# A float64-weight repair moved from VectorE to ScalarE, and a tile of their own for the first two chunks' results

## The chip, the cores and the metric

The kernel runs on one core of one Trainium2 chip. The metric is device time in microseconds (us) of one execution. Three executions of the kernel before took 899.41, 894.22 and 908.81 us, so the median is 899.41 us. The engines are TensorE (PE, with its weight loads as PEld), VectorE (DVE), ScalarE (ACT), GpSimd (POOL) and SyncE (SP), which issues most DMAs. Each runs its own instructions strictly in the order in which the program holds them.

## The reference

Three stages are chained. `S` is 576, the head dimension 64, with 4 batches of 8 heads; the 2304 tokens have 512 columns.

```python
# 1. attention: a pooled one (mean over 4 positions) and a local one (|i - j| < 4), added
out_d = sm_attn(q_d, k_d, v_d); out_up = np.repeat(out_d, 4, axis=2)
scores = np.where(mask, scale * q @ k.T, -1e9); out_local = softmax(scores) @ v
x = (out_up + out_local) as rows of (2304, 512)
# 2. a dense layer with a gate, w_in (512, 2048), w_out (2048, 512)
h = x @ w_in
g = np.where(h >= 1, h, np.where(h <= -1, 0.0, (h + 1) ** 2 / 4))
x = g @ w_out
# 3. eight experts: tokens are given out greedily by logits = x @ w_gate, 288 to each
for e in range(8):
    out[mask_e] = np.maximum(x[mask_e] @ w1[e], 0) @ w2[e]
```

`w_in` and `w_out` arrive as float64. Each is turned into float32 on the chip, by integer work on its two 32-bit words.

## The kernel before

**Tiling.** Attention runs per pair of heads: 16 pairs, each with a pooled part (`pooled`) and two local parts (`local`, g = 0 and 1). Results go to a buffer in device memory, `x_cols`. The dense layer takes the tokens in chunks of 256: seven chunks (c = 0 to 6) and a last piece of 512. For each chunk `x_cols` is loaded into the tile `xio`, split into a rounded high part and a low part (tiles `xts0` and `xts1`, even and odd chunks), and multiplied by 16 tiles of `w_in`; gated; and multiplied by 16 tiles of `w_out`. Each product takes three matmuls, high by high, high by low, low by high. In the trace the first product reads `bk<-xts,wi` and the second `bk<-wo,ghi` and `bk<-wo,glo`. Then come the routing and the experts.

**Weights.** There are 32 weight tiles, 16 of each matrix. `prep(w, f)` makes one of them ready. `scale64` lets ACT read the high words as floats times 2^-111 into a temporary `t` (or `gar`), and lets POOL reduce the high words, in place, to their sign. DVE then takes the top three bits of the low words, ors them onto the sign, shifts `t` left by three and ors again: two integer instructions, the second and third lines of

```python
        lw, hw = words(w, f)
        V.scalar_tensor_tensor(hw, lw, 29, hw, op0=OP.logical_shift_right, op1=OP.bitwise_or)
        V.scalar_tensor_tensor(ti, ti, 3, hw, op0=OP.logical_shift_left, op1=OP.bitwise_or)
```

`parts` then lets ACT copy `t` to the rounded high part, and DVE or POOL subtract to get the low part. For `w_out`, `gate_rows` also turns the tile on PE and multiplies it by the gate's weights (`bk<-wgk,rows`).

**Chunks 0 and 1** are special: `up` and `down` run them f by f while attention and weights are still being made, with the results in four PSUM banks (second products 512 wide). `flush_first` copies a chunk's results to `xio`, sends them to `x_rows`, and multiplies them by the gate's weights. From chunk 2 on, second products are 256 and 264 wide, and the first one waits until both flushes have emptied their banks.

**What sets the order.** The program is written by a planner: the functions above are generators, and `run` picks the next step by estimated engine times and by priorities (`PRIO`). What a step waits for (a tile's slot, a bank, a mark of another step) is its `need(...)`. A step given as a dictionary of engines and costs goes to the engine that the planner takes to be cheapest. Where the planner expects PE to be idle ahead of the first chunk, it puts matmuls on a bank of no use, `bk<-cst`, to keep PE busy. The tile `xio` has one slot, and the chunks' loads and all flushes share it; ahead of chunk 0 the attention uses it as scratch space.

Lines in the trace: 120 and 124 are PE's matmuls and transposes, 128 is ACT, 141 is DVE and POOL, 106 is SP's DMA. These are helpers, so instructions are told apart by their tiles.

## Time and profile before

| | |
|---|---|
| median of three runs | 899.41 us |
| the profiled execution | 900.66 us |
| its span in the trace, first to last instruction | 898.5 us |
| PE busy | 858.7 us (96%) |
| DVE busy | 514.9 us (57%) |
| ACT busy | 463.1 us (52%) |
| POOL busy | 439.2 us (49%) |

The span is 2.2 us shorter than the time of that execution, which is 1.25 us above the median of the runs. Busy PE time includes the matmuls on the useless bank, and a matmul that runs at half clock counts as busy for twice as long. The shares are means over stages with different limits, so they are read by stretch.

### The profile page before, as it was taken

The page shows a single profiled execution, that of the slowest core. Times are in us where ns is not written, and L with a number is a line of the kernel's source. Part 1 is how long each engine was busy: PE and PEld are TensorE (multiplying, and loading weights), DVE is VectorE, ACT ScalarE, POOL GpSimd, SP SyncE. Part 2 cuts the span into 40 slices and gives each one's busy share as a digit, 9 for nine tenths or more (in the row PEclk, how much of TensorE's full clock was granted, in tenths as well). Part 3 has the DMA queues.
Part 4 walks back from the last instruction along what each step waited for, and adds up shares of the span by engine and source line. Part 5 has one row for each costly group of instructions (what it writes and reads, how often), then busy time and mean ns, then how long its engine had stood idle before and what let it go on. Part 6 is the DMA issues. An engine that isn't in the chain of part 4 may idle for free.

```text
span 898.5 us, 20588 instructions
## 1 busy us (share of the span) xinstructions
PE 858.7 (96%) x7891; PEld 777.8 (87%) x7891; DVE 514.9 (57%) x1469; ACT 463.1 (52%) x1295; POOL 439.2 (49%) x498
## 2 busy tenths in 40 slices
PE   7879999989899999999999999998999999999995
PEld 6768888878899999999999877777988998989995
DVE  6788989876454543423221564475576766767520
ACT  5877786776466666544444551032343443544641
POOL 3765477654244544444444210033855756657741
PEclk9999999999899999999999999997999999999998
DMA  9755455223222310301000000053433544436620
GB/s 308 232 176 185 139 179 194 88 61 111 89 64 70 103 42 15 95 1 49 1 25 1 30 1 6 1 207 126 145 122 128 183 140 152 150 101 209 208 84 27
DMA packets 39010, 95.41 MB, mean 106 GB/s; under 512 B 4992, under 2 KB 17152, under 8 KB 38912
## 3 DMA queue, kind: packets, MB, share of 16 engines
q1 hardware_dynamic: 35840, 84.66, 28.8%
q0 software_dynamic: 3072, 9.44, 3.4%
q8 instruction: 62, 1.02, 0.5%
q14 instruction: 36, 0.29, 0.1%
HBM read 79.92 MB, written 14.16 MB: 105 GB/s over the span
## 4 chain that ended last, share of the span: by engine, by line
PE 72%; DVE 8%; DMA 7%; issue 5%; ACT 4%; POOL 2%; SPq 1%; POOLq 0%; DVEq 0%; ACTq 0%
PE bk L120 70%; PE bk L124 3%; DMA stg<-in_w_dram 2%; DVE gar L141 1%; DMA vw<-in_vw_dram 1%; ACT gar L128 1%; DVE raw L141 1%; DMA v<-in_v_dram 1%; DMA x_rows<-xio 1%; POOL wo L141 1%; DMA x_cols<-x 1%; POOL out_dram L1116 1%; SPq L106 1%; DVE t L141 1%; DMA xg<-x_rows,idx 1%
## 5 line engine op out<-in xcount | busy, mean ns | idle before, releaser
L120 PE MATMUL bk<-xts,wi 128*128 128x256 f32 x1344 | 184.8, 288 | 5.3 <-ACT gar L128 3.7
L120 PEld LDWEIGHTS bk<-xts,wi 128*128 128x128 f32 x1344 | 170.6, 192 | 9.4 <-ACT gar L128 5.1
L120 PE MATMUL bk<-wo,ghi 128*128 128x256 f32 (+2 forms) x768 | 161.8, 309 | 0.0
L128 ACT ACTIVATE gar<-bk,halves 128x256 f32<-128x256 f32 x224 | 93.8, 471 | 91.0 <-PE bk L120 85.4
L141 DVE SCALAR_TENSOR_TENSOR gar<-gar 128x256 f32<-128x256 f32 x112 | 57.4, 513 | 115.7 <-ACT gar L128 115.4
L120 PEld LDWEIGHTS bk<-wo,ghi 128*128 128x128 f32 x768 | 115.9, 190 | 4.6 <-issue 0.4
L141 POOL TENSOR_TENSOR glo<-gar,ghi 128x256 fp32r<-128x256 f32 x86 | 65.8, 771 | 86.4 <-ACT ghi L128 71.5
L141 POOL TENSOR_TENSOR wi<-stg,wi 128x512 fp32r<-128x512 f32 x51 | 64.7, 1297 | 69.4 <-DMA stg<-in_w_dram 43.0
L120 PE MATMUL bk<-wo,glo 128*128 128x256 f32 (+2 forms) x384 | 90.3, 303 | 0.2 <-DVE glo L141 0.2
L141 POOL TENSOR_TENSOR gar<-gar 128x256 f32<-128x256 f32 x64 | 49.6, 775 | 72.4 <-DVE gar L141 47.0
L141 POOL TENSOR_TENSOR wo<-stg,wo 128x512 fp32r<-128x512 f32 x50 | 65.6, 1335 | 37.6 <-ACT wo L128 37.3
L120 PEld LDWEIGHTS bk<-wo,glo 128*128 128x128 f32 x384 | 62.1, 189 | 3.6 <-DVE glo L141 0.9
L128 ACT ACTIVATE ghi<-gar 128x256 fp32r<-128x256 f32 x112 | 46.7, 417 | 34.9 <-POOL gar L141 19.5
L120 PE MATMUL bk<-xT,wi 128*128 128x288 f32 x384 | 60.8, 311 | 0.1
L120 PE MATMUL bk<-hT,wi 128*128 128x288 f32 x384 | 60.5, 304 | 0.0
L128 ACT ACTIVATE wi<-stg 128x1024 fp32r<-128x1024 f32 x32 | 33.6, 1056 | 51.4 <-DMA stg<-in_w_dram 51.4
L120 PE MATMUL bk<-hT,wo 128*128 128x288 f32 x384 | 58.8, 302 | 0.0
L120 PE MATMUL bk<-xT,wo 128*128 128x288 f32 x384 | 58.4, 302 | 0.1
L128 ACT ACTIVATE lt<-lt,lmx 128x64 f32<-128x64 f32 x160 | 53.8, 342 | 8.9 <-DVE lmx L141 8.7
L120 PEld LDWEIGHTS bk<-xT,wi 128*128 128x128 f32 x384 | 54.4, 197 | 0.8 <-DVE xT L141 0.3
L120 PEld LDWEIGHTS bk<-xT,wo 128*128 128x128 f32 x384 | 52.0, 188 | 1.0 <-DVE xT L141 0.6
L120 PEld LDWEIGHTS bk<-hT,wi 128*128 128x128 f32 x384 | 52.1, 188 | 0.7
(189 smaller groups left out, 1669.2 us busy)
## 6 DMA issues: line engine op xcount, KB each, us to landing
stg<-in_w_dram SPq DMA_DIRECT2D x64, 512.0 KB
qk<-in_qk_dram SPq DMA_DIRECT2D x14, 590.0 KB
raw<-in_win_dram SPq DMA_DIRECT2D x16, 512.0 KB
raw<-in_wout_dram SPq DMA_DIRECT2D x16, 512.0 KB
v<-in_v_dram SPq DMA_DIRECT2D x32, 144.0 KB
xio<-x_cols SPq DMA_DIRECT2D x7, 512.0 KB
x_rows<-xio SPq DMA_DIRECT2D x7, 512.0 KB
vw<-in_vw_dram SPq DMA_DIRECT2D x16, 192.0 KB
```

Of the source, the lines that this page charges most:

```text
L106: nc.sync.dma_start(out, x)
L120: return nc.tensor.matmul(out, w, x, **kw)
L124: return nc.tensor.transpose(out, x, i)
L128: return nc.scalar.activation(out, x, f, **kw)
L141: return fn(out, *args, **kw)
L1116: return nc.gpsimd.indirect_dma_start(**kw)
```

## The change

Four things change.

1. `scale64` gets one more ACT instruction ahead of the others: it reads byte 3 of every low word, computes Relu(byte / 32 - 31/64), and writes the result, rounded to a whole number, as 16 bits over the low half of that word. POOL's sign is now written as bfloat16 over the upper half of the same word. So one DVE instruction ors both onto `t`, and the other (`raw<-raw` in the trace) is gone.
2. `parts` may put the copy to the high part on ACT or on DVE, by the costs `HI`.
3. `flush_first` writes to a tile of its own, which takes the place of `xts1` once both chunks' first products are done; `xio` is not held. Both flushes now wait for that point.
4. `load_chunks` may load chunk 2 into `xio` as soon as its rows are there, and waits with the split for chunk 0's first products; chunk 3 waits for both flushes' logits and makes a new `xts1`.

```diff
+HI = (630.0,900.0)
...
+    V.memset(less, -31.0 / 64)
...
     def scale64(w, f, t):
         _, hw = words(w, f)
         yield "A"
+
+        act(RAW[w, f].bitcast(U16).rearrange("p (a b) -> p a b", b=4)[:, :, 0],
+            RAW[w, f].bitcast(U8).rearrange("p (a b) -> p a b", b=8)[:, :, 3], AF.Relu, bias=less, scale=1.0 / 32)
         act(t, f32(hw), AF.Copy, scale=2.0 ** -111)
         yield "G"
-        G.tensor_scalar(f32(hw), f32(hw), 0.0, 1.0, op0=OP.mult, op1=OP.mult)
+        G.tensor_scalar(RAW[w, f].bitcast(BF).rearrange("p (a b) -> p a b", b=4)[:, :, 1], f32(hw), 0.0, 1.0, op0=OP.mult, op1=OP.mult)
...
-        act(hi, x, AF.Copy)
+        e = yield {"A": HI[0], "V": HI[1]}
+        if e == "A":
+            act(hi, x, AF.Copy)
+        else:
+            V.tensor_copy(hi, x)
...
-        lw, hw = words(w, f)
-
-        V.scalar_tensor_tensor(hw, lw, 29, hw, op0=OP.logical_shift_right, op1=OP.bitwise_or)
-        V.scalar_tensor_tensor(ti, ti, 3, hw, op0=OP.logical_shift_left, op1=OP.bitwise_or)
-        spawn(parts(w, f, t, n), "A")
+        lw, _ = words(w, f)
+        V.scalar_tensor_tensor(ti, ti, 3, lw, op0=OP.logical_shift_left, op1=OP.bitwise_or)
+        spawn(parts(w, f, t, n))
...
     def flush_first(c):
-        yield need("V", "xio")
-        xe = bt([128, 1024], F32, "xio").rearrange("p (t d) -> p t d", t=2)
+        yield need("V", cond=lambda: done("first", 0) and done("first", 1))
+        if "e" not in FIRST:
+            FIRST["e"] = bt([128, 2048], F32, "xts1")
+        xe = FIRST["e"][:, 1024 * c:1024 * c + 1024].rearrange("p (t d) -> p t d", t=2)
...
-        drop(xio=0)
         mark("logits", c)
...
-            yield need("N", "xio", cond=lambda: there(256 * c + 256) and (c > 1 or done("scored", 2 + c, 1)) and done("first", c - 2) and (c == 2 or done("flush", c - 2)) and (c or all(1 in spare[n] for n in ("pe", "paT"))))
+            yield need("N", "xio", cond=lambda: there(256 * c + 256) and (c > 1 or done("scored", 2 + c, 1)) and (c == 2 or done("first", c - 2) and done("flush", c - 2)) and (c != 3 or done("logits", 0) and done("logits", 1)) and (c or all(1 in spare[n] for n in ("pe", "paT"))))
...
-            if c < 2:
-                XTS[c] = bt([128, 2, 4, 256], F32R, f"xts{c}")
+            if c == 2:
+                yield need("N", cond=lambda: done("first", 0))
+            if c < 2 or c == 3:
+                XTS[c % 2] = bt([128, 2, 4, 256], F32R, f"xts{c % 2}")
```

Since the planner's costs and conditions change, it writes the attention and the first chunks in another order. From the beginning of chunk 3 (its fourth first product) on, PE's order is the same as before to the end, through the routing and the experts. Three places follow, each engine's rows as the program holds them.

**ACT ahead of chunk 0.** `raw` is a weight tile's words, `t` its temporary, `wo` and `wi` finished weights, `lt` a local part's scores, `xts` the split chunk. Before, up to the first split instruction:

```order
L128 ACTIVATE t_69<-raw_248 128x512
L128 ACTIVATE paT_696<-bk_760 72x288
L128 ACTIVATE pe_780,psm_718<-bk_692,pmx_717 96x144 x3
L128 ACTIVATE lt_0162_773,lsm_777<-lt_0162_773,lmx_776 128x64 x2
L128 ACTIVATE laT_814<-bk_785 128x256
L128 ACTIVATE lt_0162_773,lsm_777<-lt_0162_773,lmx_776 128x64 x2
L128 ACTIVATE wo_837<-t_70 128x512
L128 ACTIVATE lt_1174_818,lsm_822<-lt_1174_818,lmx_821 128x64 x4
L128 ACTIVATE po_879<-bk_869 128x144
L128 ACTIVATE wi_886<-t_69 128x512
L128 ACTIVATE xts_895<-xio_758 128x256
```

And now, up to the same point:

```order
L131 ACTIVATE lt_0194_934,lsm_938<-lt_0194_934,lmx_937 128x64 x2
L131 ACTIVATE rows_967<-bk_945 128x512
L131 ACTIVATE lt_0194_934,lsm_938<-lt_0194_934,lmx_937 128x64 x2
L131 ACTIVATE raw_530<-raw_530,halves 128x512
L131 ACTIVATE t_70<-raw_530 128x512
L131 ACTIVATE lt_1204_969,lsm_973<-lt_1204_969,lmx_972 128x64 x2
L131 ACTIVATE wo_923<-bk_979 128x8
L131 ACTIVATE w2g<-bk_979 128x8
L131 ACTIVATE lt_1204_969,lsm_973<-lt_1204_969,lmx_972 128x64 x2
L131 ACTIVATE lt_0211_1012,lsm_1016<-lt_0211_1012,lmx_1015 128x64 x2
L131 ACTIVATE xts_1036<-xio_926 128x256
```

The split has moved back. Counted over the whole program up to what the first chunk matmul needs of ACT, 115 ACT instructions have become 150, with the pairs `raw<-raw` and `t<-raw` of six further weight tiles among them (13 tiles are begun there, 7 before). The copies `wo<-t` and `wi<-t` are gone from ACT.

**PE at the first chunk matmul** (the row `xts`,`wi`). Before:

```order
L120 MATMUL bk_869<-paT_696,vs_735 64x144 x4
L120 MATMUL bk_82<-cst 128x128 x2
L124 MATMUL bk_890<-cst,t_70 128x128 x4
L120 MATMUL bk_82<-cst 128x128 x3
L120 MATMUL bk_911<-wgk_84,rows_905 128x8 x4
L124 MATMUL bk_922<-cst,lt_0162_773 128x128 x2
L124 MATMUL bk_926<-cst,pe_780 72x96 x3
L120 MATMUL bk_941<-xts_895,wi_422 128x256 x12
```

And now:

```order
L127 MATMUL bk_1111<-cst,lt_1204_969 128x128 x2
L123 MATMUL bk_83<-cst 128x128 x4
L123 MATMUL bk_1131<-laT_1123,vw_861 64x58 x6
L123 MATMUL bk_1131<-laT_1123,vw_861 64x54 x2
L123 MATMUL bk_1143<-qk_481 64x64
L123 MATMUL bk_1144<-qk_481 64x64 x2
L123 MATMUL bk_1143<-qk_481 64x64 x2
L123 MATMUL bk_1144<-qk_481 64x64 x2
L123 MATMUL bk_1143<-qk_481 64x64
L123 MATMUL bk_1153<-xts_1036,wi_256 128x256 x12
```

The last two local parts of the first batch (`laT`, `vw`) and the scores of a following pair now stand ahead of the chunk; before, they stood behind its start.

**PE between the last second product of chunks 0 and 1** (512 wide) **and the first one of chunk 2** (256 and 264 wide). Transposes that read `xio` (before) or `xts` (now) are those of the flushes. Before, behind the last 512-wide row:

```order
L120 MATMUL bk_941<-xts_895,wi_649 128x256 x12
L120 MATMUL bk_941<-xts_895,wi_723 128x256 x12
L120 MATMUL bk_3198<-wgk_84,rows_3176 128x8 x4
L124 MATMUL bk_3208<-cst,lt_0582_3067 128x128 x3
L124 MATMUL bk_3216<-cst,xio_3122 128x128 x4
L120 MATMUL bk_3233<-wgk_84,rows_3228 128x8 x4
L120 MATMUL bk_3239<-laT_3231,vw_2974 64x58 x12
L124 MATMUL bk_3261<-cst,lt_0591_3107 128x128 x2
L120 MATMUL bk_3269<-laT_3264,vw_2822 64x58 x6
L120 MATMUL bk_3269<-laT_3264,vw_2822 64x54 x2
L124 MATMUL bk_3280<-cst,xio_3254 128x128 x4
L120 MATMUL bk_3288<-wo_641,ghi_3168 128x256
```

And now, with the last 512-wide rows in front:

```order
L123 MATMUL bk_1156<-wo_2558,ghi_3031 128x512 x2
L123 MATMUL bk_1156<-wo_2558,glo_3032 128x512
L123 MATMUL bk_1157<-wo_2558,ghi_3031 128x512 x2
L123 MATMUL bk_1157<-wo_2558,glo_3032 128x512
L127 MATMUL bk_3169<-cst,lt_1538_2865 128x128 x2
L123 MATMUL bk_1153<-xts_1036,wi_756 128x256 x12
L127 MATMUL bk_3195<-cst,xts_3043 128x128 x4
L127 MATMUL bk_3200<-cst,pe_3005 72x96 x3
L127 MATMUL bk_3211<-cst,xts_3043 128x128 x4
L123 MATMUL bk_3216<-wo_418,ghi_3092 128x256
```

Before, the first flush's transposes and gate matmuls all stand ahead of chunk 2's second product, and the second flush begins only then; now both flushes follow each other at once.

## Rows read from the trace of the kernel before

**Rows 1.** Busy time by stretch, all engines; columns in the first line.

```profile
core 0: us, PE busy (x) PEld busy (x) DVE busy (x) ACT busy (x) POOL busy (x), PEclk, DMA share, GB/s
9.60:61.80 52.20, 43.02 (x577) 37.63 (x578) 42.65 (x95) 41.32 (x174) 35.18 (x47) 1.00 0.78 254
61.80:100.00 38.20, 34.68 (x357) 30.19 (x355) 34.52 (x69) 27.75 (x97) 20.80 (x25) 0.91 0.46 156
100.00:136.00 36.00, 35.81 (x344) 31.02 (x337) 31.18 (x66) 29.48 (x108) 22.40 (x27) 1.00 0.51 165
136.00:173.00 37.00, 35.96 (x305) 31.53 (x304) 33.05 (x59) 27.06 (x88) 25.13 (x27) 0.95 0.49 160
173.00:220.00 47.00, 43.49 (x412) 36.86 (x410) 37.45 (x77) 31.90 (x107) 26.75 (x30) 0.96 0.24 72
220.00:245.00 25.00, 21.59 (x206) 20.12 (x201) 9.64 (x27) 11.70 (x39) 6.68 (x10) 0.86 0.33 111
245.00:360.00 115.00, 115.00 (x1232) 109.50 (x1231) 56.96 (x141) 71.61 (x263) 53.78 (x73) 1.00 0.18 57
```

**Rows 2.** PE alone in the half-clock stretches: length, busy, granted clock, DMA.

```profile
63.10:70.00 6.90, 6.25 (x40) 0.51 0.14 46
...
230.40:237.20 6.80, 6.27 (x58) 0.50 0.48 158
sum 20.50, PE 19.32; mean PE 4.83
```

**Rows 3.** PE in order of time, at the first chunk matmul: start, duration, instruction.

```profile
61.81 0.36 PE L120 MATMUL bk<-xts,wi 128*128 128x256 f32 x1
```

**Rows 4.** Groups by shape, ACT: count, busy us, mean ns, idle before.

```profile
L128 ACT ACTIVATE wi<-stg 128x1024 fp32r<-128x1024 f32 x32 | 33.6, 1056 | 51.4 <-DMA stg<-in_w_dram 51.4
L128 ACT ACTIVATE lw<-bk,halves 128x512 f32<-128x512 f32 x32 | 20.3, 685 | 16.8 <-PE bk L120 11.5 <-POOL wi L141 5.3
L128 ACT ACTIVATE t<-raw 128x512 f32<-128x512 f32 x29 | 19.2, 674 | 0.1
L128 ACT ACTIVATE wo<-t 128x512 fp32r<-128x512 f32 x15 | 9.5, 633 | 6.7 <-DVE t L141 6.6
```

**Rows 5.** The same view, DVE.

```profile
L141 DVE SCALAR_TENSOR_TENSOR raw<-raw 128x512 int32<-128x512 int32 x32 | 29.3, 916 | 5.0 <-POOL raw L141 5.0
L141 DVE SCALAR_TENSOR_TENSOR t<-t,raw 128x512 int32<-128x512 int32 x29 | 25.4, 876 | 2.2
L141 DVE COPY xg<-bk 96x512 f32<-96x512 f32 x1 | 0.7, 686 | 13.8 <-PE bk L124 13.8
L141 DVE CAST cb<-t 128x256 bf16<-128x256 f32 x1 | 0.3, 295 | 0.1
L141 DVE CAST tp<-cst 128x18 bf16<-128x18 f32 x2 | 0.2, 164 | 0.0
```

**Rows 6.** The tile of raw weights: duration ns min/median/max.

```profile
L141 DVE SCALAR_TENSOR_TENSOR raw<-raw x32: 665/694/1797, 16.8 to 203.7; 128x512 int32<-128x512 int32 x32
```

**Rows 7.** PE in order of time, small work around chunk 0.

```profile
71.24 0.66 PE L124 MATMUL bk<-cst,t 128*128 128x128 f32 x4
...
73.26 0.67 PE L120 MATMUL bk<-laT,vw 64*64 64x58 f32 x16
73.86 1.06 PE L120 MATMUL bk<-wgk,rows 128*128 128x8 f32 x8
```

**Rows 8.** PE in order of time, from the last 512-wide product.

```profile
219.23 0.40 PE L120 MATMUL bk<-wo,glo 128*128 128x512 f32 x1
...
224.63 1.69 PE L120 MATMUL bk<-xts,wi 128*128 128x256 f32 x12 [0.93 <-ACT gar L128]
...
229.88 1.45 PE L120 MATMUL bk<-wgk,rows 128*128 128x8 f32 x8 [1.95 <-ACT rows L128]
...
235.75 0.78 PE L120 MATMUL bk<-wo,ghi 128*128 128x256 f32 x2
```

**Rows 9.** SP's DMA issues in order of time.

```profile
220.40 12.20 SPq L106 DMA_DIRECT2D x_rows<-xio  x2
```

More of the change, by code (lines that the diff above doesn't have):

```diff
@@ L14 @@
 BF = mybir.dt.bfloat16
+U16 = mybir.dt.uint16
+U8 = mybir.dt.uint8
 I32 = mybir.dt.int32
@@ L180, in body @@
     w2g = P.tile([128, 16, 2, E], F32R, name="w2g")
-    halfs = P.tile([128, 2], F32, name="halves")
-    half, mhalf = halfs[:, 0:1], halfs[:, 1:2]
+    halfs = P.tile([128, 3], F32, name="halves")
+    half, mhalf, less = (halfs[:, i:i + 1] for i in range(3))
+    V.memset(less, -31.0 / 64)
     V.memset(half, 0.5)
```

## The prediction, made before the changed kernel was run

> **What bounds the kernel now.** I read the busy time by stretch first. From 245 to 360 us PE is busy for 115.00 of 115.00 us at full clock [rows 1], and every other engine has room. So in the chunks PE sets the pace, and since PE's order is unchanged from the start of chunk 3, a shift that exists there reaches the end one to one. The change can act only ahead of that point, about 245 us by these stretches. There the reader should see two regimes. Up to 61.8 us, where the first chunk matmul starts [rows 3], PE has little real work and waits for the attention and the weights; DVE is busy 42.65 and ACT 41.32 of 52.20 us [rows 1], 82% and 79%. From 61.8 to 245 us PE is busy 171.5 of 183.2 us (the five rows' sum), so 11.7 us are idle. It also ran at half clock for 20.5 us, 19.3 of them busy [rows 2]; at full clock that work would have taken 9.7 us less. Together 21.3 us between 61.8 and 245 us are not PE's work at full speed. That is all that a smoother middle can give back, and the start of the chunks is the other lever.
>
> The sum is made against the profiled execution, 900.66 us, which is 1.25 us above the median of the three runs.
>
> **The weight repair and the copy.** DVE loses 32 instructions of 916 ns [rows 5]: 29.3 us. It gains the copy in 29 of 32 tiles. No such copy is in the trace; the nearest rows are a conversion of 256 elements, 295 ns, and one of 18, 164 ns [rows 5]. That is 0.55 ns an element, so 512 take about 0.43 us; the bounds are 295 and 686 ns (a copy of 512 out of PSUM [rows 5]). So 12.5 us come back (8.6 to 19.9), and DVE is relieved by about 17 us. ACT gains 32 byte readings. Nearest is a gate instruction with the same function, a bias column and 512 elements: 685 ns [rows 4], 21.9 us. A plain reading of the same strided words, 674 ns, is the lower bound; an ACT instruction of 1024 elements, 1056 ns, the upper one (bytes at half rate), which would add 11.9 us. ACT loses 29 copies of 633 ns, 18.4 us. Net +3.5 us. POOL's sign instruction keeps its elements; I cost the narrower writing at nothing, since each tile's chain still has ACT's two readings beside it.
>
> So no engine that runs at 80% is freed for nothing: the work moves from DVE to ACT. What matters more is the order that the planner made of it.
>
> **The chunks start later.** The changed order puts 13 weight tiles ahead of the first chunk matmul where 7 stood, besides two local parts and the scores of a pair. ACT must do 150 instructions instead of 115. Of the 35 more, 13 are byte readings (8.9 us), 6 readings of words (4.0 us), and 6 copies fall away (-3.8 us); the other 22, among them six exponentials that count twice in the trace for their sums, are 28 trace instructions at this stretch's mean of 41.32/174 = 0.24 us: 6.6 us. Sum 15.7 us; at ACT's 79% that takes 19.8 us. If instead ACT's 10.9 idle us took them first, 4.8 us would be left. DVE goes from 97 to 127: 7 raw instructions less (-6.4), 6 second ones more at 876 ns (+5.3), 11 copies (+4.7), and 19 others at the stretch's mean of 42.65/95 = 0.45 us (8.5): 12.1 us, at 82% 14.8 us. I take **+16 us** for the start (4.8 to 19.8): near DVE's value, since ACT has a little more idle time to give.
>
> Against this stands the PE work that now lies ahead of the start. Two weight tiles turned and multiplied for the gate: 2 x (0.66 + 1.06) us; two local value products: 2 x 0.67 us [rows 7]; these durations overlap their neighbours a little. 28 small score matmuls and nine others take about as much again as the value products. **-6 us**.
>
> **The flush.** Between the end of the last 512-wide product (219.6 us) and chunk 2's first second product (235.75 us) lie 16.1 us [rows 8]. In 220 to 245 PE is idle 3.4 us [rows 1], the longest of it 1.95 us for ACT's copy of the flush's transposes [rows 8], and 6.8 us run at half clock [rows 2], which costs 3.1. SP too is held for 12.2 us over the two issues of `x_rows`, with loads queued behind [rows 9]. In the new order one first product and two groups of transposes lie between. The flushes' copies still have to be made, so I leave 1.5 us: **-5 us** (0 to -6.5). What is late next is chunk 2's gates, as before.
>
> **The middle.** 14.8 of the 21.3 us remain. From 61.8 to 220 us DVE is busy 136.2 of 158.2 us, 86% [rows 1]. From that go the 17 us of relief and the 12 us that now lie ahead of the start, and about 4 come back for subtractions that the planner moved from POOL to DVE: 111 us, some 70%, are left. ACT has 12 us less to do there. PE waits for both, so I take half of the loss: **-7.5 us** (0 to -14.8).
>
> Sum: +16 - 6 - 5 - 7.5 = -2.5, so 898.2 us for the profiled execution, and 1.25 us less for a median: **897 us**. With every term at its best end it is 877, at its worst 913.
>
> **A rule against the change.** DVE's removed instruction took 694 ns in the median and 1797 at most, 916 in the mean [rows 5, 6]: some of its kind are stretched to more than twice. 32 x 0.22 = 7 us of DVE's time is such stretching. The Trainium skill says under "Who interferes with whom" (page "SBUF — State Buffer") that a DVE copy in a two-port mode and a GpSimd instruction exclude each other for the whole instruction, and that a DVE instruction with two SBUF inputs collides with GpSimd's reads. By that rule the stretched row fits, and the new copies on DVE lock POOL out where ACT's did not; it is a rival below.
>
> **The rivals.**
> 1. *The late start is not paid back* (slower). Place: the first chunk matmul, behind six more weight tiles on ACT. Price: 19.8 - 6 = +13.8, the flush gives 2, the middle nothing: +11.8, **911 us** by the median. It decides if idle and half-clock loss after the start stays above 15 us. For it: once PE is the bound, PE time lost at the front is gone. Against: ACT and DVE were both near 85% and now have less to do. Chance 0.20.
> 2. *The front packs well* (faster). More tiles in flight fill ACT's and DVE's idle 20% ahead of the start: +8 - 6 - 6 - 12 = -16, **883 us**. Against: waits of 2 us for PE results are part of each chain. Chance 0.15.
> 3. *The flush's own tile does nothing*: chunk 2 waits for its gates all the same. -5 becomes 0: **902 us**. For it: one of the waits in that place, 0.93 us, ends on ACT's gate work [rows 8]. Chance 0.10.
> 4. *DVE's copies hold POOL up.* 29 x 0.43 = 12.5 us of held POOL, all on chains that PE waits for: **909 us**. POOL is busy 54 to 68% in these stretches [rows 1]. Against: the removed 29 us held it too, for longer each. That is the rule above. Chance 0.05.
> 5. *The forecast*, 890 to 903: 0.50.
>
> Two per cent of the median is 18 us, about what a measurement of this kernel can tell from no change: under 881 is faster, over 917 slower. No case's centre lies there. Beyond rival 2's centre lies the best end, 877: 0.05. Beyond rival 1's lie 913 and a byte reading at 1056 ns, which adds 11.9 us on ACT: 0.06. So 0.89 stays for no change. The range takes in rivals 1 and 2: **884 to 911 us**.
>
> **What the changed profile would show.** The first `xts`,`wi` matmul at 76 to 80 us instead of 61.8. The byte reading at about 0.69 us and DVE's copy at about 0.43 us. Less than 5 us between the last 512-wide product and the first 256-wide one. PE's idle and half-clock loss from the start to chunk 3 down from 21 to about 9 us. The forecast is wrong if the start moves by less than 8 us, if the byte reading takes over 1 us, or if the loss in the middle stays.

## The result: 1.4% slower, and the profile after

The changed kernel takes 913.68 us (median of four executions, 905.29 to 915.98) against 898.85 us for the kernel before on the same chip: ratio 1.0141, 95% interval 1.0097 to 1.0185. The ratio is estimated from all these executions; the quotient of the two medians is 1.0165. The forecast was 897 us with a range from 884 to 911. The profiled execution is the slowest of the four, 915.98 us; its span is 914.2 us. In the experiments below the medians leave out two executions that lie far above the others, one of e2 (2028.72 us) and one of e6 (1336.41 us).

First the busy time by stretch, in the stretches of [rows 1] and with their columns:

```profile
9.60:61.80 52.20, 43.59 (x496) 38.23 (x498) 39.22 (x77) 45.79 (x158) 38.77 (x45) 0.94 0.75 248
61.80:100.00 38.20, 34.08 (x339) 30.79 (x336) 25.81 (x65) 26.69 (x93) 20.15 (x19) 0.77 0.54 178
100.00:136.00 36.00, 32.97 (x305) 28.18 (x305) 32.32 (x58) 29.47 (x74) 22.59 (x23) 0.95 0.37 123
136.00:173.00 37.00, 34.03 (x307) 29.35 (x299) 29.29 (x65) 31.59 (x97) 24.12 (x25) 1.00 0.39 137
173.00:220.00 47.00, 45.55 (x424) 39.61 (x425) 39.51 (x82) 37.07 (x121) 30.63 (x31) 1.00 0.24 78
220.00:245.00 25.00, 25.00 (x247) 21.99 (x245) 12.64 (x34) 16.43 (x60) 10.09 (x15) 1.00 0.40 126
245.00:360.00 115.00, 114.83 (x1260) 108.87 (x1258) 59.39 (x143) 71.63 (x265) 52.54 (x72) 1.00 0.20 65
```

From 61.8 to 100 us, where the chunks have not begun until 89 us, PE's granted clock is 0.77 instead of 0.91. From 100 to 173 us PE is busy 67.0 of 73 us instead of 71.8. From 220 to 245 us PE is never idle and at full clock, where it was idle 3.4 us at 0.86. From 245 us PE is full again, as before. PE alone, in its longest half-clock stretch (length, busy, clock, DMA):

```profile
65.50:82.60 17.10, 16.68 (x125) 0.50 0.50 170
```

It answers [rows 2], where the stretch at this place was 6.9 us long. The largest group in it now is the products on the bank of no use:

```profile
L123 PE MATMUL bk<-cst 128*128 128x128 f32 x31 | 8.7, 440 | 0.0
```

The first chunk matmul answers [rows 3] (start, duration):

```profile
89.00 1.70 PE L123 MATMUL bk<-xts,wi 128*128 128x256 f32 x12
```

So the start is 27.2 us later, not 16. The groups by shape of the changed kernel, for ACT, DVE and POOL ([rows 4, 5]), say why:

```profile
L131 ACT ACTIVATE raw<-raw,halves 128x512 uint16<-128x512 uint8 x32 | 46.5, 1454 | 0.1
L131 ACT ACTIVATE t<-raw 128x512 f32<-128x512 f32 x28 | 20.0, 713 | 0.0
...
L144 DVE SCALAR_TENSOR_TENSOR t<-t,raw 128x512 int32<-128x512 int32 x28 | 24.6, 879 | 1.6 <-POOL raw L144 1.2
L144 DVE CAST wi<-t 128x512 fp32r<-128x512 f32 x13 | 9.3, 714 | 0.1
L144 DVE CAST wo<-t 128x512 fp32r<-128x512 f32 x12 | 5.7, 473 | 0.1
...
L144 POOL TENSOR_SCALAR raw<-raw 128x512 bf16<-128x512 f32 x32 | 44.6, 1421 | 21.3 <-ACT raw L131 21.3
```

And POOL's sign instruction in the same view of the kernel before:

```profile
L141 POOL TENSOR_SCALAR raw<-raw 128x512 f32<-128x512 f32 x32 | 23.6, 744 | 7.1 <-ACT t L128 5.7 <-DMA qk<-in_qk_dram 1.1 <-ACT gar L128 0.2
```

ACT's byte reading takes 1454 ns, not 685, and POOL's sign, on the same 512 elements, 1421 instead of 744 ns. Both now write 16-bit elements at steps of 8 bytes. POOL's idle time before the sign ends with the byte reading, so the sign runs behind it and beside ACT's other reading of the tile, 0.71 us. At the flush, PE in order of time (answers [rows 8]):

```profile
237.62 0.40 PE L123 MATMUL bk<-wo,glo 128*128 128x512 f32 x1
...
239.50 0.60 PE L127 MATMUL bk<-cst,xts 128*128 128x128 f32 x4
...
240.54 0.48 PE L123 MATMUL bk<-wo,ghi 128*128 128x256 f32 x2
```

Between the starts of the last 512-wide product and the first 256-wide one lie 2.9 us instead of 16.5. SP's issues of `x_rows` are now no longer than its others (0.38 us each, against 12.20 for the two in [rows 9]):

```profile
230.38 0.38 SPq L109 DMA_DIRECT2D x_rows<-xts  x1
...
239.36 0.38 SPq L109 DMA_DIRECT2D x_rows<-xts  x1
```

Of what the prediction said the profile would show, two things came. The gap at the flush is under 5 us, and PE's idle and half-clock loss from the start to chunk 3 fell from 21.3 to 10.6 us (8.9 idle, 1.7 for 3.4 us at half clock), near its 9. The start (76 to 80 us), the byte reading (0.69 us) and DVE's copy (0.43 us, now 18.2 us for 29, so 0.63) missed, and a byte reading of over 1 us was one of its signs of being wrong.

### The profile page after: what moved, and what is told of

It reads as the page before. It is cut to its first block, busy times and chain, and to the rows that moved or that the text cites. A ratio compares the mean times of both kernels' runs of the same rounds, so it can differ in the third digit from the quotient of the medians.

```text
span 914.2 us, 20696 instructions
## 1 busy us (share of the span) xinstructions
PE 871.5 (95%) x7947; PEld 789.7 (86%) x7947; DVE 513.6 (56%) x1472; ACT 485.6 (53%) x1298; POOL 452.0 (49%) x493
## 4 chain that ended last, share of the span: by engine, by line
PE 64%; issue 7%; POOL 7%; DVE 7%; DMA 7%; ACT 6%; SPq 0%; POOLq 0%; ACTq 0%; DVEq 0%
PE bk L123 61%; DMA stg<-in_w_dram 4%; PE bk L127 3%; POOL raw L144 2%; POOL wi L144 2%; POOL wo L144 1%; ACT raw L131 1%; DVE t L144 1%; DVE wi L144 1%; ACT lt L131 1%; ACT gar L131 1%; POOL out_dram L1129 1%; DMA x_rows<-xio 1%; POOL v L144 1%; DVE gar L144 1%
## 5 line engine op out<-in xcount | busy, mean ns | idle before, releaser
L123 PE MATMUL bk<-xts,wi 128*128 128x256 f32 x1344 | 181.8, 285 | 4.9 <-ACT gar L131 4.7
L123 PEld LDWEIGHTS bk<-xts,wi 128*128 128x128 f32 x1344 | 167.4, 189 | 9.2 <-ACT gar L131 7.4
L144 DVE SCALAR_TENSOR_TENSOR gar<-gar 128x256 f32<-128x256 f32 x112 | 54.6, 488 | 116.8 <-ACT gar L131 116.8
L144 POOL TENSOR_TENSOR glo<-gar,ghi 128x256 fp32r<-128x256 f32 x81 | 61.9, 771 | 67.0 <-ACT ghi L131 66.4
L144 POOL TENSOR_TENSOR gar<-gar 128x256 f32<-128x256 f32 x67 | 51.7, 772 | 85.6 <-DVE gar L144 60.7
L144 POOL TENSOR_SCALAR raw<-raw 128x512 bf16<-128x512 f32 x32 | 44.6, 1421 | 21.3 <-ACT raw L131 21.3
```

What stands on the lines that cost most here:

```text
L123: return nc.tensor.matmul(out, w, x, **kw)
L144: return fn(out, *args, **kw)
```

## The experiments

Each run is timed beside the kernel before on the same chip. Below, "start" is the first `xts`,`wi` matmul, "flush end" the first 256-wide product, both in the profiled execution (before: 61.81 and 235.75 us; the change: 89.00 and 240.54).

| run | repair | copies | flush's own tile | order | median us | ratio (95%) | start | flush end |
|---|---|---|---|---|---|---|---|---|
| e1 | as the change, both writings 32-bit | 29 on DVE | yes | change's | 900.83 | 0.9967 (0.9939 to 0.9996) | 80.44 | 223.73 |
| e2 | only ACT's writing 32-bit | 29 on DVE | yes | change's | 916.17 (three runs) | 1.0172 (1.0101 to 1.0242) | 88.41 | 242.18 |
| e5 | only POOL's writing 32-bit | 29 on DVE | yes | change's | 904.43 | 1.0005 (0.9972 to 1.0039) | 81.84 | 228.09 |
| e3 | as before | 21 on DVE | yes | own | 907.09 | 1.0033 (0.9994 to 1.0072) | 70.19 | 240.73 |
| e7 | as before | ACT | yes | own | 893.62 | 0.9854 (0.9817 to 0.9891) | 62.87 | 224.60 |
| e12 | as before | 21 on DVE | no | own | 906.34 | 1.0062 (1.0038 to 1.0087) | 70.19 | 247.05 |
| e11 | as before | ACT | yes | e3's | 900.67 | 0.9969 (0.9932 to 1.0006) | 62.91 | 230.13 |
| e9 | as the change | ACT | yes | own | 910.11 | 1.0090 (1.0059 to 1.0121) | 70.97 | 241.32 |
| e8 | as the change | DVE | yes | own | 916.84 | 1.0111 (1.0078 to 1.0144) | 67.61 | 248.67 |
| e6 | sign 32-bit, then byte | 21 on DVE | yes | own | 902.29 | 0.9983 (0.9959 to 1.0007) | 73.02 | 231.19 |
| e10 | sign 32-bit, then byte | ACT | yes | own | 921.59 | 1.0194 (1.0150 to 1.0239) | 71.38 | 256.16 |
| e13 | as before (e7 again) | ACT | yes | e7's | 890.46 | 0.9885 (0.9856 to 0.9914) | 65.37 | 224.53 |
| e14 | as before, sign in 16 bits | ACT | yes | e7's | 907.00 | 1.0075 (1.0050 to 1.0101) | 64.64 | 234.89 |
| e15 | as before | DVE | yes | e7's | 903.85 | 1.0027 (1.0005 to 1.0050) | 63.78 | 233.23 |
| e16 | DVE's first instruction gone | ACT | yes | e7's | 880.25 | 0.9764 (0.9729 to 0.9799) | 62.80 | 213.33 |
| e17 | e16 and the byte reading | ACT | yes | e7's | 900.67 | 0.9982 (0.9952 to 1.0012) | 68.60 | 234.38 |
| e18 | as the change | DVE | yes | e7's | 910.35 | 1.0091 (1.0052 to 1.0129) | 65.39 | 236.40 |

**The two writings, in the change's own order (e1, e2, e5).**

```diff
 # ACT, 32-bit (e1, e2); POOL, 32-bit (e1 over hw, e5 over lw)
-act(<16 bits of lw>, <byte 3 of lw>, AF.Relu, bias=less, scale=1.0 / 32)
+act(<the word lw>, <byte 3 of lw>, AF.Relu, bias=less, scale=1.0 / 32)
-G.tensor_scalar(<upper 16 bits of lw>, f32(hw), 0.0, 1.0, ...)
+G.tensor_scalar(f32(hw), f32(hw), 0.0, 1.0, ...)
```

> The changed kernel, every instruction in the same order, but ACT writes its byte reading as 32-bit whole numbers over the low word and POOL writes the sign as 32-bit floats over the high word, as before. It leaves out the sign of the weights. Theory W (the 16-bit writes with a stride of 8 bytes are what costs): ACT's byte reading falls from 1.45 to about 0.69 us and POOL's sign from 1.42 to 0.74; the first chunk matmul comes at 76 to 80 us instead of 89, and the time is 896 to 903, as forecast. Rival O (the order costs: thirteen weight tiles ahead of the chunks): the durations may fall, but the start stays at 84 or later and the time at 908 to 914. Rival B (reading single bytes costs): ACT's instruction stays at 1.45 us.

> The changed kernel in the same order, with only ACT's byte reading written as 32-bit whole numbers; POOL still writes 16 bits of sign onto the upper half of the same word, and nothing is left out. Theory W: ACT's instruction 0.69 us, POOL's still 1.42; start at 80 to 85 us, time 902 to 909. Rival B: ACT's stays at 1.45 us and nothing moves. Rival O: the durations may fall, the time stays within 4 us of the changed kernel.

> The changed kernel in its own order; only the sign instruction on POOL writes 32-bit words again (a float over the whole low word), while the byte reading on ACT keeps its 16-bit writing at 1.45 us. Left out by it: the low three bits of the weights. Theory A (POOL's 16-bit writing, 1.42 instead of 0.74 us, is what holds the weights up, ACT's is beside the path): POOL's sign takes 0.75 us, the first chunk matmul starts at 79 to 82 us as with both writings wide (80.4), and the time is 899 to 905 us, ratio 0.995 to 1.001. Rival B (either slow instruction alone is enough, since the chain of a tile holds both): the start stays at 86 to 89 us and the time at 914 to 920, ratio 1.012 to 1.018. Rival C (half each): start at 84 to 85, 907 to 911 us.

The groups by shape, of e1:

```profile
L131 ACT ACTIVATE raw<-raw,halves 128x512 int32<-128x512 uint8 x32 | 24.6, 767 | 0.1
L144 POOL TENSOR_SCALAR raw<-raw 128x512 f32<-128x512 f32 x32 | 23.9, 750 | 19.9 <-ACT t L131 18.6 <-ACT gar L131 1.2
```

of e2:

```profile
L144 POOL TENSOR_SCALAR raw<-raw 128x512 bf16<-128x512 f32 x32 | 44.2, 1417 | 15.4 <-ACT raw L131 15.3
```

and of e5:

```profile
L131 ACT ACTIVATE raw<-raw,halves 128x512 uint16<-128x512 uint8 x32 | 46.7, 1458 | 0.1
L144 POOL TENSOR_SCALAR raw<-raw 128x512 f32<-128x512 f32 x32 | 22.4, 701 | 25.7 <-ACT raw L131 25.4 <-PE bk L123 0.2
```

With both writings wide the start is at 80.4 us and the kernel is 0.3% faster than before, 3.4 us, where the forecast for the change was 2.5 us. But e1 changes more than the widths. Its sign lies in the high word, which DVE's one instruction does not read, so DVE no longer waits for it: six of the 32 instructions begin before the sign of their tile is done. In the changed kernel DVE's longest waits for the sign stood before the four tiles in `gar`:

```profile
L144 DVE SCALAR_TENSOR_TENSOR gar<-gar,raw 128x512 int32<-128x512 int32 x4 | 4.9, 1255 | 5.3 <-POOL raw L144 5.3
```

and in e1 neither group of this instruction waits for POOL:

```profile
L144 DVE SCALAR_TENSOR_TENSOR t<-t,raw 128x512 int32<-128x512 int32 x28 | 23.2, 828 | 0.4 <-ACT t L131 0.4
...
L144 DVE SCALAR_TENSOR_TENSOR gar<-gar,raw 128x512 int32<-128x512 int32 x4 | 3.9, 991 | 0.0
```

e5 keeps the wait, since its sign goes over the low word. ACT's width alone changes nothing (e2 missed its expectation of 902 to 909 us); POOL's alone brings the start to 81.8 us and the ratio to 1.0005. So in this order the whole miss goes with POOL's writing: 1.0141 - 1.0005 = 1.4%, 12 us, and the two intervals do not overlap. From e2 to e1, where ACT writes words, it is 1.0172 - 0.9967 = 2.1%, but that holds the lost wait as well.

**What is dear in the byte reading (e4).** One execution of the change with four forms of ACT's instruction, eight tiles each (bytes or words read, 16 or 32 bits written; low bits of the weights are wrong in the two forms that read words).

```diff
-act(<16 bits of lw>, <byte 3 of lw>, ...)
+src = f32(hw) if f % 2 else <byte 3 of lw>
+dst = <the word lw> if f % 4 > 1 else <16 bits of lw>
+act(dst, src, ...)
```

> The changed kernel in the same order, with four forms of ACT's extra instruction by the tile's number: reading bytes or reading 32-bit floats (the high word; the low bits are then wrong), writing 16 or 32 bits, all with a stride of 8 bytes. Theory W: the two forms that write 16 bits take 1.4 to 1.5 us, the two that write 32 bits about 0.7. Rival B: the two that read bytes take 1.45, the two that read floats 0.7.

Groups by shape, ACT:

```profile
L131 ACT ACTIVATE raw<-raw,halves 128x512 uint16<-128x512 uint8 x8 | 11.6, 1450 | 0.0
L131 ACT ACTIVATE raw<-raw,halves 128x512 uint16<-128x512 f32 x8 | 11.6, 1449 | 0.0
L131 ACT ACTIVATE raw<-raw,halves 128x512 int32<-128x512 f32 x8 | 6.2, 772 | 0.0
L131 ACT ACTIVATE raw<-raw,halves 128x512 int32<-128x512 uint8 x8 | 6.1, 766 | 0.0
```

Reading bytes costs nothing (766 against 772 ns); writing 16 bits at a step of 8 bytes costs 680 ns more than writing 32 bits at the same step.

**The flush and the copy apart (e3, e7, e12, e11).** e7 is the kernel before with the new `flush_first` and `load_chunks`; e12 the kernel before with the choice of engine for the copy; e3 has both, with the old repair; e11 is e3 in its own order, but with each copy issued on ACT:

```diff
         else:
-            V.tensor_copy(hi, x)
+            spend("V", V.fixed + 0.5 * V.per * size(x))
+            nc.scalar.activation(hi, x, AF.Copy)
```

> The changed kernel with the weight repair of before (two DVE instructions, POOL's sign as 32-bit floats, no byte reading); the flushes' own tile and the copy on ACT or DVE stay. The planner then puts 7 weight tiles ahead of chunk 0, as before. Theories W and O both: the start is back at 60 to 64 us; with the flush's gain of 5 us the time is 891 to 898. If the flush or the copies on DVE were what costs (rival F): 905 or more.

> The kernel before with the flush's own tile and the new loading conditions alone; repair and copies as before. Prediction's reading (the flush held chunk 2 up by some 5 us): the gap between the last 512-wide product and the first 256-wide one falls from 16 to 3 to 7 us, and the time to 897 to 901 us, ratio 0.991 to 0.997. Rival F (chunk 2 waits for work on ACT and PE that is only moved ahead of it): the gap is shorter, the last 512-wide product comes later by the same time, and the time stays within 2 us of the kernel before, ratio 0.998 to 1.002.

> The kernel before with the choice of engine for the copy alone (21 copies on DVE, 11 on ACT); repair and flush as before. Theory I and rival J alike put its cost at what the old repair with the choice and the flush had over the flush alone, 13 to 16 us: first 256-wide product at 246 to 252 us, 912 to 919 us, ratio 1.010 to 1.018. Rival K (the copy costs only where the flush's own tile is there too): 902 to 906 us, ratio 0.998 to 1.003.

> The kernel with the old repair, the flush's own tile and the choice for the copy (1.003 of the kernel before, first 256-wide product at 240.7 us), with the order that the planner made of it, but the 21 copies that it gave to DVE are issued on ACT at the same places of the program. Theory I (DVE's instructions themselves hold it up: DVE is busy 112.7 of 118.2 us between 61.8 and 180 us there): DVE's busy time in that stretch falls to about 104, the first 256-wide product comes at 226 to 232 us and the time is 892 to 899 us, ratio 0.986 to 0.993. Rival J (the order is what costs): DVE has room, the product is still at 237 to 243 us, and the time is 904 to 910, ratio 1.000 to 1.006.

The flush's own tile is the gain, 1.5%; rival F fell. The copy's choice takes it all back: e3 was expected at 891 to 898 us and stands at 907. Of that 1.8%, 0.6% goes with the place of the copies (1.0033 to 0.9969 in the same order, with intervals that overlap) and the rest with the order that the planner makes once it may choose (0.9854, or 0.9885 in e13, to 0.9969, with intervals that do not); theory I and rival J may each have a part. Alone the choice costs 0.6%, less than either expected, though more than nothing.

**Other orders of the change (e8, e9, e6, e10).**

```diff
 # e8: the planner is told the narrow writings' price
+        spend("A", 800.0)
+        spend("G", 700.0)
 # e9: copies stay on ACT
-        spawn(parts(w, f, t, n))
+        spawn(parts(w, f, t, n), "A")
 # e6 (e10: with e9's edit): sign first, in words over hw; then the byte into hw's low half
-        act(<16 bits of lw>, <byte 3 of lw>, ...)
         act(t, f32(hw), AF.Copy, scale=2.0 ** -111)
-        G.tensor_scalar(<upper 16 bits of lw>, f32(hw), ...)
+        G.tensor_scalar(f32(hw), f32(hw), ...)
+        act(<low 16 bits of hw>, <byte 3 of lw>, ...)
```

> The changed kernel, its instructions unchanged, but the planner is told what the two narrow writings cost (0.8 us more on ACT and 0.7 us more on POOL for each tile). It then puts the first chunk matmul at row 129 of PE's order instead of 157, with 6 or 7 weight tiles ahead of it instead of 13, and makes all 32 copies on DVE. Theory A (the dear writings cost mostly because 13 tiles stand ahead of the chunks): start at 66 to 74 us, time 903 to 909 us, ratio 0.999 to 1.005. Rival D (what is not waited for ahead of the start is waited for behind it, since the weights' pace is POOL's and ACT's): the start is as early, but the 193rd chunk matmul is not before 154 us and the time is 912 to 920, ratio 1.009 to 1.018.

> The changed kernel without the choice of engine for the copy: all 29 copies stay on ACT, as before; its repair with the narrow writings and its flush are as changed. The planner then puts the first chunk matmul at row 133 of PE's order. Theory A (the narrow writing on POOL is the dear part, and it costs at any order): weights' 13th tile no later than in the changed kernel, start 64 to 72 us, the first 256-wide product 5 to 12 us later than with the flush alone (224.6), so 230 to 237, and the time 899 to 906 us, ratio 0.995 to 1.004. Rival G (the copies' place on DVE and the order that the planner makes of it are the dear part, as the old repair with the choice, at 1.003, against the flush alone, at 0.985, lets one think): first 256-wide product at 222 to 227 us, 891 to 897 us, ratio 0.983 to 0.991.

> The changed kernel with the two instructions of the repair in another place: POOL puts the sign over the high word in 32-bit words, as the kernel before does, and then ACT's byte reading writes its 16 bits into that word's low half. All of the result is computed. The planner makes its own order of it, with the first chunk matmul at row 136 of PE's order instead of 157. Theory A: POOL's sign at 0.75 us, ACT's byte reading still 1.45 us, start at 68 to 76 us, time 898 to 905 us, ratio 0.993 to 1.001. Rival B (ACT's narrow writing, now last in the chain of a tile ahead of DVE, holds the weights up as POOL's did): the weights' 13th tile not before 85 us and the time 908 to 916, ratio 1.005 to 1.014.

> The kernel with POOL's sign in 32-bit words ahead of ACT's byte reading, and with all copies on ACT: 32 byte readings of 1.45 us and 29 copies of 0.63 us on ACT, nothing of the removed 29 us left on DVE. All of the result is computed. Theory A: POOL's price is gone, so it is as fast as the flush alone or faster, 888 to 895 us, ratio 0.982 to 0.988. Rival H (ACT is then what is late: 46 us of byte readings are added to it in the first 212 us): the weights' 13th tile not before 105 us, first 256-wide product at 230 to 240 us, 899 to 908 us, ratio 0.994 to 1.004.

In e8 the start moves from 89 to 67.6 us and the kernel is no faster: the 13th weight tile's second repair instruction is at 115.5 us instead of 86.6, the flush end at 248.7. So an early start alone wins nothing back; rival D holds in the time, though the 193rd chunk matmul came at 145.2 us, earlier than it said. In e9 the narrow repair with all copies on ACT, in the planner's own order, costs 2% on top of the flush alone; its flush end is at 241.3 us. Rival G fell with it, and theory A's 899 to 906 us was too low. e6 has theory A's time (with POOL's narrow writing gone all of the result comes at 0.998), but rival B's mark too: the 13th tile is at 103.3 us. e10 shows the other engine: with byte readings and copies both on ACT the 13th tile is at 120.3 us, and the kernel is the slowest of all, beyond what rival H gave.

**One order, one edit at a time (e13 to e18).** From e3 on, the order mostly moved with the edit. Here every engine keeps e7's order (the planner is told the old costs) and one thing is changed (in e17 a second, in e18 all).

```diff
 # e14: POOL
-        G.tensor_scalar(f32(hw), f32(hw), 0.0, 1.0, ...)
+        nc.gpsimd.tensor_scalar(<upper 16 bits of hw>, f32(hw), 0.0, 1.0, ...)
 # e15
-        act(hi, x, AF.Copy)
+        nc.vector.tensor_copy(hi, x)
 # e16
-        V.scalar_tensor_tensor(hw, lw, 29, hw, ...)
 # e17: e16, and
+        nc.scalar.activation(<16 bits of lw>, <byte 3 of lw>, AF.Relu, ...)
```

> The kernel with the flush's own tile alone once more, in more rounds, as the base of the three that follow. If the 13 us of its four runs hold: 889 to 896 us, ratio 0.981 to 0.989. If they were an accident of four runs, and the 4 to 6 us hold by which its profiled execution was ahead of the kernel before at the later marks: 895 to 899 us, ratio 0.991 to 0.997.

> The flush alone, every engine's order unchanged, only POOL's sign is written in 16 bits over the upper half of the high word; left out is the clearing of the lower half, so low bits of the weights are wrong. Theory A (POOL's 1.42 instead of 0.74 us holds the weights up): weights' 13th tile at 102 to 108 us instead of 96, first 256-wide product at 232 to 240 us instead of 224.6, 8 to 16 us slower than the flush alone in the same call. Rival J (the narrow writing costs only by the order that stands with it): within 3 us of the flush alone, POOL's sign at 1.42 us all the same.

> The flush alone, the order of the work unchanged, but all 32 copies are issued on DVE at the places where ACT made them, with the old repair. Theory I (DVE's instruction itself holds DVE and so PE up; DVE is busy 105.5 of 118.2 us between 61.8 and 180): a copy takes 0.47 to 0.71 us, DVE 110 to 116 us of that stretch, 5 to 10 us slower than the flush alone. Rival J (the order costs 10 of the 16 us and the instruction little): 0 to 4 us slower.

> The flush alone, the order unchanged, without DVE's first repair instruction and with nothing in its place; left out are the low three bits of the weights. It shows what DVE's relief, 29 us of instructions, is worth by itself. Prediction's reading (PE waits for DVE in the middle: half of 14.8 us and some of the start comes back): start 55 to 60 us, 6 to 14 us faster than the flush alone, 879 to 888 us. Rival L (DVE's instructions are beside the path, or what is late next is ACT and POOL): within 3 us of the flush alone.

> The flush alone without DVE's first repair instruction, in the same order, and with ACT's 32 byte readings (16-bit writing) ahead of its readings of the high words; their result is not used, so the low three bits of the weights are still left out. The base is the same without the byte readings, 0.9764 of the kernel before. Theory M (ACT, at 88 of 118 us between 61.8 and 180, has the room: the byte reading is the cheapest of the edits): 880 to 885 us, ratio 0.976 to 0.983. Rival H (46 us more on ACT ahead of 212 us hold the weights up, as where the sign came first and all copies stood on ACT, at 1.019): ACT over 104 us of that stretch, weights' 13th tile 10 us later than without, 890 to 905 us, ratio 0.989 to 1.005.

> All of the change's instructions in the order of the flush alone: narrow byte reading on ACT, narrow sign on POOL, no first repair instruction on DVE, and all copies on DVE. All of the result is computed. The prices measured one by one in this order are -10 us for the flush, -10 for DVE's instruction, +16.5 for the narrow sign, +13.4 for the copies on DVE: +10 us and the byte reading's own price. Theory N (the prices add up, the planner's order with 13 tiles ahead of the start gives and takes nothing): 910 to 918 us, ratio 1.010 to 1.019, near the changed kernel's 1.014. Rival O (the order with 13 tiles ahead costs): under 904 us. Rival P (that order wins something back, the edits together are worse): over 922 us.

Busy time from 61.8 to 180 us (columns as in [rows 1]) of e13, the base:

```profile
61.80:180.00 118.20, 113.79 (x1100) 99.27 (x1099) 107.62 (x206) 89.50 (x303) 74.59 (x86) 0.98 0.49 163
```

of e14, the narrow sign, +16.5 us:

```profile
61.80:180.00 118.20, 107.07 (x1011) 92.95 (x1009) 108.40 (x194) 85.69 (x291) 81.03 (x79) 0.97 0.49 161
```

of e15, the copies on DVE, +13.4 us:

```profile
61.80:180.00 118.20, 110.10 (x1023) 95.13 (x1024) 110.83 (x215) 76.77 (x274) 69.86 (x81) 0.97 0.47 158
```

of e16, DVE's first repair instruction gone, -10.2 us:

```profile
61.80:180.00 118.20, 115.42 (x1135) 101.84 (x1135) 91.36 (x195) 93.36 (x319) 75.97 (x87) 0.98 0.49 161
```

of e17, the byte reading added to e16, 2.2% or +20 us:

```profile
61.80:180.00 118.20, 109.26 (x1029) 94.19 (x1029) 80.93 (x175) 103.21 (x301) 64.53 (x77) 0.95 0.50 162
```

and of e18, all of the change's instructions:

```profile
61.80:180.00 118.20, 108.60 (x1005) 93.45 (x1001) 96.05 (x192) 94.78 (x282) 76.88 (x78) 0.96 0.50 162
```

PE's busy time, the first figure behind the length, is the higher the lower the ratio, but for two neighbouring pairs (e17 and e15, e14 and e18). DVE is busy 107.6 of 118.2 us in the base, and the edits that load it or make it wait cost; taking 32 instructions off it is worth 10 us (the start, at 62.8 us, did not come as early as the 55 to 60 expected). POOL is busy only 69% in e14 and its narrow writing still costs 16.5 us, just above theory A's 8 to 16. The cost is not at the start (64.6 us, 65.4 in e13), and the 13th tile, at 98.4 us, is earlier than theory A's 102 to 108. DVE's wait for `raw` goes from 5.3 to 9.4 us, and its first instruction takes 4.0 us more in all beside the narrow sign (below); no run tells what each of the two is worth. The profiled executions show half of the 16.5 us (902.04 and 894.05 us): e14's is the fastest of its ten, e13's the slowest of its six. The copies in e15 cost more than theory I's 10 us. ACT in e17 is at 103 us, just under rival H's 104, and its 13th tile 12 us later than in e16 (101.7 against 89.6). e18 says that the prices do not add up. They come to 0.9885 + 0.019 + 0.014 - 0.012 + 0.022 = 1.031 and the measured ratio is 1.009. It fits that the copies on DVE leave ACT room for the byte reading (ACT 94.8 us instead of 103.2), and that the removed instruction leaves DVE room for the copies (96.1 instead of 110.8), but no run shows this apart. Theory N's 910 us was reached only at its lower edge, and by luck: its sum left the byte reading's 20 us open. The change's own order, 1.0141, is not told apart from e18's 1.0091 by their intervals.

## Why the prediction was wrong, step by step

**The step that failed** is the one on the repair: "POOL's sign instruction keeps its elements; I cost the narrower writing at nothing, since each tile's chain still has ACT's two readings beside it." The instruction went from 744 to 1421 ns, and it lies in each tile's chain behind ACT's byte reading and ahead of DVE's instruction, which waits for it. Of ACT's two readings only the second runs beside it, and that takes 0.71 us. In the change's order undoing it alone (e5) is worth 1.4%, in the flush's order making it alone (e14) costs 16.5 us. No bounds were given for it, so the range lacked its cost altogether. This is enough for the miss: without it (e5) the time is 904.4 us, on a chip where the kernel before took 902.9. Whether the sign costs by what waits for it or by what it slows on DVE stays open.

**The byte reading** was taken at 685 ns and bounded at 1056 by a slower reading of bytes. It takes 1454, and the reason is the writing (e4), which had no bound. In the change's order, where most copies have left ACT, those 0.77 us a tile cost between nothing (e2 against the change) and 0.4% (e5 against e1, which lacks DVE's wait too). In e17, with the copies on ACT, the whole reading cost 2.2%.

**The start.** Forecast +16 us, 4.8 to 19.8; measured +27.2. With both writings wide it is +18.6, inside the bounds and nearer to the sum for ACT (19.8) than to that for DVE (14.8), by which the forecast went. POOL's writing makes 7 to 8 us of the rest (89.00 - 81.84, and 88.41 - 80.44 with the lost wait in it) and ACT's about 1. For the 13 tiles ahead of the start POOL's 13 x 0.677 = 8.8 us says the same.

**The PE work ahead and the middle** were put at -6 and -7.5. From the start to the last 512-wide product the kernel before takes 157.4 us, e1 140.4, the change 148.6. With wide writings the terms' 13.5 us are there (17.0); with the narrow ones 8.8, and both now have flush work within that stretch (the first `x_rows` is issued at 213.6 and 230.4 us). DVE's relief is real: 10.2 us in e16. The 29 copies of 512 elements took 18.2 us in all (25 in the two rows above and four of other tiles, 3.2), inside the 8.6 to 19.9.

**The flush** was too small: -5 us, at most 6.5, against -9.9 us by e13's medians (0.9885) and -9.3 by e7's (ratio 0.9854). In the profiled e13 the gap falls to 2.2 us, with the last 512-wide product 3.1 later: 11.2 us ahead at the flush end. Part of that is only moved: at the first `XTL` product it is 5.8 us ahead (484.92 against 490.73), near the forecast. The medians show some 4 us more; e13's profiled execution, 894.05 us, is the slowest of its six and 3.6 us above their median.

**One to one.** The prediction let a shift at about 245 us reach the end unchanged. From one place in chunk 3 on, PE's instructions follow each other alike in both kernels. That place, before:

```profile
298.35 0.40 PE L120 MATMUL bk<-wo,ghi 128*128 128x256 f32 x2
```

and in the change:

```profile
308.50 0.49 PE L123 MATMUL bk<-wo,ghi 128*128 128x256 f32 x2
```

There the change is 10.2 us late, and 10.6 at the first `XTL` product, so through the chunks the shift does stay. The 4.8 us at the flush end are no measure of it: from there to the first `XTL` product e7, e13 and e1 take 5 to 11 us more than the kernel before as well, so it seems that work done in the gap before is done later now. From the start to this place the change takes 219.5 us instead of 236.5, 17.0 less, where the forecast's other three terms come to 18.5. So of the 12.7 us between the forecast's -2.5 and the 10.2 measured there, 11.2 are the start's. At the end of the span the change is 15.7 us late. The last 5 us lie behind the chunks, in work that no edit touches: from the first `xT` product to the end it takes 281.7 us before, 287.4 in the change, and 280.0 (e14, e15) to 285.3 (e2) elsewhere.

**The rivals.** Rival 1's 911 us is nearest to the result, but by luck. It was to be decided by a loss of over 15 us after the start, and the loss is 10.6; its terms had the start at 19.8, not 27.2. And e8 shows that an early start with nearly the same instructions is no better. What is late is the weights' chain: with 13 tiles ahead of the start that shows at the start, in e8 and e14 behind it. Its argument that ACT and DVE were both near 85% fits DVE alone: from 61.8 to 220 us ACT was busy 116.2 of 158.2 us [rows 1], 73%. Rival 2's well-packed front was not there. Rival 3 fell. Rival 4 put the copies on DVE at 12.5 us, and in one fixed order they cost 13.4; its mechanism is not seen, though. The 24 POOL instructions next to copies in e15 take 21.3 us in all, and the same 24 in e13 20.7; POOL's busy time from 9.6 to 245 us is 139.1 us in e15 against 140.7. DVE is what gets longer.

**The rule on shared ports.** The Trainium skill ("Who interferes with whom", page "SBUF — State Buffer") has a DVE copy in a two-port mode and a GpSimd instruction exclude each other. No run here shows POOL held by it, nor whether these copies run in such a mode. Its other half, that a DVE instruction with two SBUF inputs collides with GpSimd's reads, agrees with the rows that follow.

## What to carry to other kernels

Cost an instruction by the width of what it writes as much as by its elements: here 16 bits written at a step of 8 bytes doubled it on two engines, against 32 bits at the same step, and slowed a third beside it. An instruction on an engine that is only two thirds busy can cost nearly all that it grows by when it lies in a chain that a nearly full engine waits for: in e14 POOL's signs take 20.8 us more and the kernel 16.5. And where a planner orders the work, run each edit in one fixed order and alone: the part that gained here (the flush's own tile, 0.9885 by itself, faster than both kernels) was hidden by those that lost.

## What the runs showed of the hardware

**Strided 16-bit writing.** Steps of 8 bytes, 128x512: ACT 766 to 772 ns for words and 1449 to 1468 for 16 bits; POOL 670 to 757 and 1365 to 1443 (means of the runs). No run writes 16 bits at another step, so width and step are not told apart.

**POOL's narrow writing slows DVE beside it.** e13 and e14 have the same order; DVE's first repair instruction and POOL's sign by shape, in e13:

```profile
L141 DVE SCALAR_TENSOR_TENSOR raw<-raw 128x512 int32<-128x512 int32 x32 | 28.4, 887 | 5.3 <-POOL raw L141 5.3
...
L141 POOL TENSOR_SCALAR raw<-raw 128x512 f32<-128x512 f32 x32 | 23.0, 724 | 8.8 <-ACT t L128 6.8 <-DMA qk<-in_qk_dram 1.1 <-ACT gar L128 0.6
```

and in e14, where POOL's sign is the narrow one:

```profile
L141 DVE SCALAR_TENSOR_TENSOR raw<-raw 128x512 int32<-128x512 int32 x32 | 32.4, 1011 | 9.5 <-POOL raw L507 9.4
...
L507 POOL TENSOR_SCALAR raw<-raw 128x512 bf16<-128x512 f32 x32 | 43.8, 1420 | 4.4 <-ACT t L128 3.7 <-ACT gar L128 0.7
```

Set against POOL's instructions one by one, those with none beside them take 683 ns on average in e13 (8 of 32) and 685 in e14 (6). Those that run for over 30% of their length beside a sign instruction take 958 in e13 (6) and 1486 in e14 (7). Whether the narrow sign slows DVE more while it lasts, or only lasts longer, is not told apart. One such pair of e14, in order of time on POOL:

```profile
122.87 2.51 POOL L507 TENSOR_SCALAR raw<-raw 128x512 bf16<-128x512 f32 x2
125.21 0.74 POOL L141 TENSOR_TENSOR glo<-gar,ghi 128x256 fp32r<-128x256 f32 x1
128.03 1.65 POOL L141 TENSOR_TENSOR wo<-t,wo 128x512 fp32r<-128x512 f32 x1 [2.08 <-ACT wo L128]
```

and on DVE:

```profile
124.26 2.23 DVE L141 SCALAR_TENSOR_TENSOR raw<-raw 128x512 int32<-128x512 int32 x1 [0.17 <-POOL raw L507]
...
126.53 0.69 DVE L141 SCALAR_TENSOR_TENSOR t<-t,raw 128x512 int32<-128x512 int32 x1
```

The instruction that starts beside POOL's second sign lasts 2.23 us; the next one of that size, which falls into a time without POOL work (125.95 to 128.03 us), takes 0.69. The 32 conversions of 512 elements on DVE in e15 take 417 ns with no POOL instruction beside them (16) and 592 beside one that is no sign (14): the forecast's 0.43 us was the undisturbed value. The nine that begin while a POOL instruction runs take 798 ns on average, the seven in which a POOL instruction begins later 403.
